# Four copies moved from ScalarE to VectorE, one scaling moved the other way, and a running maximum joined with its new rows, at the end of an attention with soft MoE slots

## The chip, the cores and the metric

The kernel runs on one core of a Trainium2 chip. What counts is the device time of one launch in microseconds. A profiled execution gives, beside its own time, a span: from its first to its last instruction on the core.

## The reference

The inputs are q, k and v of shape (8, 12, 448, 64), a matrix phi of 768 x 32, and the weights w1 (8 experts, 768 x 1024) and w2 (8 experts, 1024 x 768), all float32. What is computed, cut to what matters:

```python
scores = scale * np.matmul(q, k.transpose(0, 1, 3, 2))
m = np.max(scores, axis=-1, keepdims=True)
e = np.exp(scores - m)
attn = e / (np.sum(e, axis=-1, keepdims=True) + np.exp(-m) + 1e-09)
attn_out = np.matmul(attn, v)
x = attn_out.transpose(0, 2, 1, 3).reshape(B * S, H * D)      # 3584 x 768

logits = x @ phi                                              # 3584 x 32
d = np.exp(logits - logits.max(0, keepdims=True))             # over all tokens
d /= d.sum(0, keepdims=True) + 1e-09
slot_input = (d.T @ x).reshape(E, S_per_e, D)                 # 8 experts, 4 slots each
for e in range(E):
    slot_out[e] = np.maximum(slot_input[e] @ w1[e], 0.0) @ w2[e]
c = np.exp(logits - logits.max(1, keepdims=True))             # over the slots
c /= c.sum(1, keepdims=True) + 1e-09
out = c @ slot_out
```

The maximum over all tokens is kept as a running maximum from batch to batch, as in an online softmax.

## The kernel before, in words

The 12 heads of each of the 8 batches are taken two at a time. So there are 48 pairs of heads, numbered 0 to 47, six to a batch (`PB`), three to a group (`NP`). One pair has 448 queries and keys in chunks of 128, 128, 128 and 64; the last half chunks of the two heads share one tile of 128 partitions, one head in each half.

The main loop (L658) runs over the pairs s, with two halves y = 0 and 1. The order of the instructions is written out by hand: each engine does its instructions in the order in which the program issues them. For a pair n:

- `A` and `A1` (L247, L271) compute scores and take their maxima over keys on VectorE (L280, L269), several pairs ahead. `W1`, `W2` and `W3` (L283, L305, L313) negate the maxima of a group on GpSimd (L286), transpose them on TensorE (L309, L310) and copy them to the tile `mT` (L315). `W3` also computes the exponentials of the negated maxima (L318, L321).
- `AB` (L354) computes scores again, transposed: `scores(1)`, `scores(0)` (L366), then `less(1)`, `less(0)` subtract the maxima by a second product with `mT` (L370), and ScalarE takes the exponential (L372). `Bk` (L325) does the same for the half chunk (L344, L347, L350).
- `AV` (L393) multiplies the exponentials with v (L405). Column 64 of every slot of its result is the sum of the exponentials. For pair s, key chunks 0 and 1 are done in its own half y = 1, the rest in the next pair's half y = 0.
- `N1` (L411) copies the result from PSUM to `ubuf` (L417). `N2` (L420) divides: sum and reciprocal on VectorE (L426, L427), then three operations that scale into the tile x: chunks 0 to 2 (L431), the reciprocal spread over two columns of which a mask `halfm` keeps one in each half of the partitions (L435), and the half chunk, with zeros in the other head's columns (L436). From pair 44 on (`on_pool` false) all of it is on VectorE, before that the copy is on ScalarE and the scaling on GpSimd. The last pair is scaled straight from PSUM.
- `PX` (L450) transposes x by four products with the identity (L457) and copies the result to `xT` (L463). In the loop `PX(s - 2)` comes in the half y = 1, after the batch's step of that half. For the last pair it uses two banks and two copies, L460 on ScalarE and L461 on VectorE.

PSUM has three pools: `psA` (three banks: maxima, and the batches' steps), `psB` (four banks, taken in turn by `AB`, `Bk`, `W2`, `PX`), `psV` (one bank, for `AV`).

`P(b)` (L470) is the soft MoE part of batch b, in steps that are put into the dictionary `post` and issued in the halves of later pairs: logits (`l_mm`, L483; copy L496), their maxima over slots (`c_max`, L500), a transposed copy and its maximum over tokens (`l_turn`, L510), `s_max` (a product with the identity spreads the maxima over all partitions, L520; reduction over the four chunks, L521; joined with the old running maximum, L523), `d_sub` (L527), exponentials (L532), the correction of the old sums (`corr`, L537; `fade`, L542), the weighted sums (`s_mm`, L551; `s_add`, L565), and `c_turn` (L556 to L561). For batch 6, the last but one, five steps lie in the second half of pair 43, the two of pair 44 and the two of pair 45.

For the last batch the steps come after the loop: `last[0]` computes logits and transposed logits (`t_mm`, L491) from chunks 0 to 3 of `xT`, `last[1]` from chunk 4, and `last[2]` from chunk 5, after which it does all the rest up to the slots' inputs. In between stand `N1(47)`, `N2(47)`, `PX(46)` and `PX(47)` (L742 to L754). `keep_busy` (L443) issues products whose results are not used.

Then come the experts: `hidden` (L764), `turn`, `slots`, `pick`, and the output's products and scalings (L814 to L879). Weights are loaded by GpSimd's and SyncE's queues during the pairs (`load_half`, `load_first` L131, `load_second` L141), some of them into space that the attention gives free at its end.

Of the kernel before, what the change touches and what calls it, by code (L numbers as in the profile page):

```python
# [8 lines left out]
F32 = mybir.dt.float32  # L9
BF16 = mybir.dt.bfloat16  # L10
AX = mybir.AxisListType
# [20 lines left out]
def kernel(  # L32
# [10 lines left out]
    nc = tc.nc  # L43
# [99 lines left out]
    with ExitStack() as at:  # L143
# [168 lines left out]

        def W3(g):  # L313
            t = psm.tile([128, S], BF16, tag="mT", name="mT")
            nc.scalar.copy(t, st["ps_m"][:, 0:S])  # L315
            mT[g] = t
            e = psm.tile([128, NP, 7], F32, tag="ec", name="ec", bufs=3)
            nc.scalar.activation(e[:, :, 0:6].rearrange("p l (i h) -> p i l h", i=3),  # L318
                                 ngm[g][:, 0:18].rearrange("p (i l h) -> p i l h", i=3, h=2),
                                 AF.Exp, scale=scale)  # L320
            nc.scalar.activation(e[:, :, 6], ngm[g][:, 18:21], AF.Exp, scale=scale)  # L321
            ec[g] = e
# [97 lines left out]
        def N2(n):  # L420
            g, pl = divmod(n, NP)
            b, pb = divmod(n, PB)
            u = us[n]
            eng = nc.gpsimd if on_pool(n) else nc.vector
            rec = psm.tile([128, 7], F32, tag="rec", name="rec", bufs=3)
            nc.vector.scalar_tensor_tensor(rec, u[:, :, D], 1e-9, ec[mg(n)][:, pl, :], op0=ALU.add, op1=ALU.add)  # L426
            nc.vector.reciprocal(rec, rec)  # L427
            x = xb[b % 2]
            c = pb * 128
            rec2 = psm.tile([128, 2], F32, tag="rec2", name="rec2", bufs=3)  # L430
            eng.tensor_mul(  # L431
                x[:, 0:3, c:c + 128].rearrange("p i (h d) -> p i h d", h=2),
                u[:, 0:6, 0:D].rearrange("p (i h) d -> p i h d", h=2),
                rec[:, 0:6].rearrange("p (i h) -> p i h", h=2).unsqueeze(3).to_broadcast([128, 3, 2, D]))
            eng.tensor_scalar(rec2, halfm, rec[:, 6:7], None, op0=ALU.mult)  # L435
            eng.tensor_mul(  # L436
                x[:, 3, c:c + 128].rearrange("p (h d) -> p h d", h=2),
                u[:, 6, 0:D].unsqueeze(1).to_broadcast([128, 2, D]),
                rec2.unsqueeze(2).to_broadcast([128, 2, D]))
# [3 lines left out]
        def keep_busy(n):  # L443

            if "idle" not in st:
                st["idle"] = pb_("ps_idle")
            for _ in range(n):
                nc.tensor.matmul(st["idle"], ident, w_sb["w1", 0][:, 0, 0:512], start=True, stop=True)

        def PX(n):  # L450
            b, pb = divmod(n, PB)
            x, c = xb[b % 2], slice(pb * 128, pb * 128 + 128)
            two = n == NPAIR - 1
            pss = [pb_("ps_x") for _ in range(1 + two)]
            for i in range(4):
                o = (i % 2 if two else i) * 128
                nc.tensor.matmul(pss[i // 2 if two else 0][:, o:o + 128], x[:, i, c], ident if i < 3 else ident2,  # L457
                                 start=True, stop=True)
            if two:
                nc.scalar.copy(xT[:, pb, 0:256], pss[0][:, 0:256])  # L460
                nc.vector.tensor_copy(xT[:, pb, 256:512], pss[1][:, 0:256])  # L461
            else:
                nc.scalar.copy(xT[:, pb, :], pss[0])  # L463

# [3 lines left out]
        def P(b):  # L470
# [7 lines left out]
            def l_mm(js):  # L478
                if js[0] == 0:
                    v["ps_l"] = pa([128, 4, NS], F32, "ps_l")  # L480
                for j in js:
                    for i in range(4):
                        nc.tensor.matmul(v["ps_l"][:, i, :], xT[:, j, i * 128:(i + 1) * 128], phi_sb[:, j, :],  # L483
                                         start=(j == 0 and i == 0), stop=(j == KC - 1), skip_group_check=True)
# [29 lines left out]
            def c_sub():  # L514
                eng.tensor_sub(v["z"][:, 0:4, :], l[:, 0:4, :],
                               v["cm"].unsqueeze(2).to_broadcast([128, 4, NS]))

            def s_max():
                ps = pa([128, 128], F32, "ps_bc")
                nc.tensor.matmul(ps, v["sm"].to_broadcast([128, 128]), ident, start=True, stop=True)  # L520
                nc.vector.reduce_max(new, ps.rearrange("p (i s) -> p s i", i=4), axis=AX.X)  # L521
                if b:
                    nc.vector.tensor_max(new, new, l[:, 4, :])  # L523

            def d_sub():
# [59 lines left out]
            if b < B - 1:  # L585
                steps = [both(lambda: l_mm(range(KC)), l_ev, c_max), both(l_turn, c_sub), both(s_max, d_sub),
                         both(exps, corr), both(s_mm, fade, s_add), c_turn]
                return steps if b < B - 2 else steps[:4] + [both(*steps[4:])]
            return [lambda: (l_mm(range(PB - 2)), t_mm(range(PB - 2))),
                    lambda: (l_mm([PB - 2]), t_mm([PB - 2])),  # L590
                    both(lambda: l_mm([PB - 1]), lambda: t_mm([PB - 1]), l_ev, l_turn, lambda: keep_busy(1), s_max,
                         d_sub, lambda: exps(4, 8), corr, lambda: keep_busy(4), fade, s_last, c_max, c_sub,
                         lambda: exps(0, 4)),
                    c_turn]
# [63 lines left out]
        for s in range(NPAIR):  # L658
            for y in range(2):
                hs = 2 * s + y  # L660
                early = int(hs < 5)
                if early:
                    As(1)
                    Bk(s, 2 * y)
                    As(1)
                    Bk(s, 2 * y + 1)
                    As(1)
                elif s < NPAIR:
                    AB(s, 2 * y)
                    if y:  # L670
                        Bk(s, 3, 1)
                    else:
                        AB(s, 1)
                if hs == 1:
                    W1(1)
                if hs < 5:
                    T(hs + 3)
                if y == 0:
                    if 0 <= s - 1:
                        for i in (2, 3):  # L680
                            AV(s - 1, i, range(3))
                else:
                    if 2 <= s < NPAIR - 6:
                        T(s + 6)
                    g = (s + 1) // 3
                    if (s + 1) % 3 == 0 and g < NG:
                        W2(g + 1)
                        W3(g + 1)
                    if s < NPAIR:
                        for i in (0, 1):  # L690
                            AV(s, i, range(3))
                if 2 * s + y in post:
                    post[2 * s + y]()
                if hs == 2 * (NPAIR - 2) + 1:
                    nc.vector.reduce_max(fold, ident.rearrange("p (i s) -> p s i", i=4), axis=AX.X)
                if y and 0 <= s - 2 < NPAIR - 2 and s - 2 != n6:
                    PX(s - 2)
                if hs == 2 * n6 + 4:
                    PX(n6)
                if y == 0:  # L700
                    if 0 <= s - 1:
                        for i in range(4):
                            AV(s - 1, i, [3])
                        N1(s - 1)
                        if not on_pool(s - 1):
                            N2(s - 1)
                else:
                    if 0 <= s - 1 and on_pool(s - 1):
                        N2(s - 1)
                As(early)  # L710
                if hs == 1:
                    W2(1)
                    W3(1)
                if hs == 4:
                    W1(2)
            g = (s + 10) // 3
            if s == 1 or s % 3 == 2:
                g = 3 if s == 1 else g
                if (s == 1 or g > 3) and g < NG:
                    load(g, "q")  # L720
                    load(g, "k")
            g = (s + 9) // 3
            if s % 3 == 0 and g - 2 < NG:
                V(g - 2)
                if s and g - 1 < NG:
                    load(g - 1, "v")
            if s % 3 == 1:
                if 1 < (s + 2) // 3 < NG:
                    W1((s + 2) // 3 + 1)
                if s == 1:  # L730
                    load(2, "v")
            if s in half_at:
                load_half(half_at[s], 0, w_tile(half_at[s]))
            if s - 2 in half_at:
                load_half(half_at[s - 2], 1)
            if s in narrow_at:
                narrow(narrow_at[s])
            for i, z0, z1 in part_at.get(s, ()):
                load_part(i, z0, z1)
            for i, z0, z1 in col_at.get(s, ()):  # L740
                load_first(i, z0, z1)
# [168 lines left out]
```

## Time and profile before

| | |
|---|---|
| median of 3 runs | 307.56 us (307.03 to 309.63) |
| the profiled execution, its own time | 307.67 us |
| its span | 305.9 us |
| TensorE busy | 274.5 us, 5077 matmuls |
| VectorE busy | 257.0 us, 608 instructions |
| ScalarE busy | 249.7 us, 552 instructions |
| GpSimd busy | 202.8 us, 400 instructions |
| mean granted TensorE clock | 0.963 (1.00 from 230 to 280 us) |

Times in the profile count from the start of the span. Busy time of TensorE is modelled, so that 90% is not its peak. PE is TensorE, DVE VectorE, ACT ScalarE, POOL GpSimd, SP SyncE; PEld is the load of weights into TensorE. A line of the timeline gives start, duration, engine, line of the program, operation, tiles and shapes; in brackets stands how long the engine had been idle before, and what ended it. The duration of an instruction holds a tail in which the next one has already begun, so the distance from start to start is shorter.

### The profile page before, as it was taken

The numbers are of one execution on the slowest core, as the hardware profiler recorded it, in microseconds if no ns is written. First come the engines' busy times: TensorE is split into PE (matmuls) and PEld (weight loads), VectorE is DVE, ScalarE is ACT, GpSimd is POOL, SyncE is SP. The second block draws the span as 40 slices with busy tenths as digits, with TensorE's granted clock in tenths as the row PEclk, the third lists the DMA queues.
The fourth block names the chain that finished last, engine by engine and source line by source line (L and its number), as shares of the span: only waits on it lengthen the run. The fifth ranks groups of instructions, "written<-read, shape, count | busy, mean of one in ns | idle before, by whom it ended". The sixth has DMA issues, their size and how long they took to land.

```text
span 305.9 us, 12225 instructions
## 1 busy us (share of the span) xinstructions
PE 274.5 (90%) x5077; PEld 157.9 (52%) x5078; DVE 257.0 (84%) x608; ACT 249.7 (82%) x552; POOL 202.8 (66%) x400
## 2 busy tenths in 40 slices
PE   7878999999999999999999999999999899994810
PEld 3334565566566656555666556556565555441200
DVE  5989999999999999989999999999999476536930
ACT  2656799999999999989999999999999997335810
POOL 8692788888698869877889697979584862000000
PEclk9999999999999999999999999999999999999555
DMA  6999999999999999998999999999962899927997
GB/s 84 156 149 197 131 207 145 208 182 191 169 192 174 189 181 182 169 204 142 134 170 187 176 189 180 176 189 201 162 90 35 137 135 210 343 106 274 410 441 315
DMA packets 49350, 57.44 MB, mean 188 GB/s; under 512 B 2832, under 2 KB 41488, under 8 KB 48912
## 3 DMA queue, kind: packets, MB, share of 16 engines
q0 software_dynamic: 45536, 42.52, 90.7%
q1 hardware_dynamic: 3760, 14.16, 11.6%
q8 instruction: 39, 0.64, 0.8%
q14 instruction: 15, 0.12, 0.1%
HBM read 88.18 MB, written 14.16 MB: 335 GB/s over the span
## 4 chain that ended last, share of the span: by engine, by line
PE 47%; DVE 27%; POOL 8%; ACT 7%; issue 5%; DMA 2%; DVEq 0%; POOLq 0%
DVE mx L280 14%; PE ps_av L405 11%; PE ps_a L278 6%; PE ps_b L366 5%; PE ps_t L234 4%; PE ps_b L370 4%; PE ps_b L344 3%; DVE mx L269 2%; DMA R<-in_v_dram 2%; DVE W L824 2%; PE ps_x L457 2%; PE ps_so L787 2%; PE ps_h L771 2%; DVE mx L260 2%; DVE R L239 2%
## 5 line engine op out<-in xcount | busy, mean ns | idle before, releaser
L280 DVE TENSOR_REDUCE mx<-ps_a 128x1 f32<-128x448 f32 x252 | 138.9, 614 | 5.4 <-PE ps_a L278 5.1
L372 ACT ACTIVATE R<-ps_b 128x448 bf16<-128x448 f32 x272 | 130.8, 571 | 0.8 <-PE ps_b L370 0.5
L278 PE MATMUL ps_a<-R 64*128 64x448 bf16 x252 | 82.1, 352 | 2.0 <-DVE mx L280 1.8
L366 PE MATMUL ps_b<-R 64*128 64x448 bf16 x272 | 74.2, 353 | 0.9
L370 PE MATMUL ps_b<-mT,sel 64*128 64x448 bf16 x272 | 70.9, 350 | 0.0
L405 PEld LDWEIGHTS <-R 128*128 128x128 bf16 (+1 forms) x1536 | 50.2, 100 | 30.4 <-issue 26.3
L405 PE MATMUL ps_av<-R 128*128 128x65 bf16 (+1 forms) x1536 | 64.5, 196 | 0.0
L431 POOL TENSOR_TENSOR R<-ubuf,rec 128x384 bf16<-128x384 f32 x44 | 36.4, 827 | 35.7 <-DVE rec L427 18.8
L350 ACT ACTIVATE R<-ps_b 128x448 bf16<-128x448 f32 x64 | 35.6, 576 | 3.3 <-PE ps_b L347 3.3
L234 PEld LDWEIGHTS <-R 64*64 64x64 bf16 x1344 | 29.7, 110 | 14.6 <-issue 6.1
L463 ACT CAST R<-ps_x 128x512 bf16<-128x512 f32 x47 | 28.1, 597 | 6.2 <-PE ps_x L457 6.2
L234 PE MATMUL ps_t<-ident,R 64*64 64x64 bf16 x1344 | 31.0, 194 | 1.7 <-DMA R<-in_k_dram 0.4
L269 DVE TENSOR_REDUCE mx<-ps_a 128x1 f32<-128x448 f32 x48 | 29.6, 616 | 0.0
L370 PEld LDWEIGHTS <-sel 64*128 64x128 bf16 x272 | 21.5, 94 | 14.6 <-issue 5.0
L278 PEld LDWEIGHTS <-R 64*128 64x128 bf16 x252 | 23.6, 94 | 10.0
L417 ACT COPY ubuf<-ps_av 128x455 f32<-128x455 f32 x44 | 25.2, 573 | 3.0 <-PE ps_av L405 2.8
L237 ACT COPY R<-ps_t 128x896 bf16<-128x896 bf16 x20 | 18.4, 922 | 9.0 <-PE ps_t L234 8.7
L260 DVE TENSOR_REDUCE mx<-ps_a 128x1 f32<-128x448 f32 x36 | 20.5, 618 | 3.6 <-PE ps_a L256 3.4
L344 PE MATMUL ps_b<-R 64*64 64x448 bf16 (+1 forms) x112 | 21.6, 371 | 0.0
L347 PE MATMUL ps_b<-mT,sel 64*64 64x448 bf16 (+1 forms) x112 | 20.4, 349 | 0.1
L436 POOL TENSOR_TENSOR R<-ubuf,rec 128x128 bf16<-128x128 f32 x44 | 17.6, 400 | 3.7
L366 PEld LDWEIGHTS <-R 64*128 64x128 bf16 x272 | 17.3, 94 | 4.7 <-issue 0.2
(136 smaller groups left out, 456.1 us busy)
## 6 DMA issues: line engine op xcount, KB each, us to landing
W<-in_moe_w_dram POOLq DMA_DIRECT2D x22, 768.0 KB, 9.6
R<-in_v_dram POOLq DMA_DIRECT2D x32, 192.0 KB, 5.2
out_dram<-W SPq DMA_DIRECT2D x2, 2688.0 KB, 10.3
R<-in_q_dram POOLq DMA_DIRECT2D x15, 336.0 KB, 7.2
R<-in_k_dram POOLq DMA_DIRECT2D x15, 336.0 KB, 8.1
wd<-in_moe_w_dram POOLq DMA_DIRECT2D x8, 384.0 KB, 10.2
R<-wd SPq DMA_DIRECT2D x8, 384.0 KB, 8.4
R<-in_moe_w_dram POOLq DMA_DIRECT2D x2, 768.0 KB, 9.2
```

The source lines that it names most:

```text
L234: nc.tensor.transpose(ps[r, a, c:c + 64], src[r, pl, tok * D:(tok + 1) * D], ident[r, r])
L269: nc.vector.reduce_max(mx[g][:, c:c + 1], ps[:, 0:S], axis=AX.X)
L278: nc.tensor.matmul(ps[:, 0:S], t[r, 0, i * 128:(i + 1) * 128], t[r, 1, :], start=True, stop=True)
L280: nc.vector.reduce_max(mx[g][:, c:c + 1], ps[:, 0:S], axis=AX.X)
L344: nc.tensor.matmul(outs[hl], t[rs[hl], 1, cols], t[rs[hl], 0, :], start=True, stop=False)
L350: nc.scalar.activation(e, p[:, 0:S], AF.Exp, scale=scale)
L366: nc.tensor.matmul(ps[hl][:, 0:S], t[rs[hl], 1, cols], t[rs[hl], 0, :], start=True, stop=False)
L370: nc.tensor.matmul(ps[hl][:, 0:S], sel[rs[hl], h:h + 1].to_broadcast([64, 128]), mT[mg(n)][rs[hl], :], start=False, stop=True)
L372: nc.scalar.activation(e[:, hl, :], ps[hl][:, 0:S], AF.Exp, scale=scale)
L405: nc.tensor.matmul(o, eT[n, i, hl][:, qc], vp[g % 2][:, 2 * pl + hl, i, 0:W65], start=(i == 0 and u == 0 and hl == 0), stop=(i == 3), skip ...
L431: eng.tensor_mul(x[:, 0:3, c:c + 128].rearrange("p i (h d) -> p i h d", h=2), u[:, 0:6, 0:D].rearrange("p (i h) d -> p i h d", h=2), rec[: ...
L463: nc.scalar.copy(xT[:, pb, :], pss[0])
```

## The change

1. `W3` of the last group (pairs 45 to 47) copies the transposed maxima (128x448) on VectorE instead of ScalarE.
2. `PX` of pairs 42, 43 and 44 copies its result (128x512) on VectorE instead of ScalarE.
3. In `N2` of the last pair, the masked reciprocal and the masked scaling of the half chunk on VectorE are replaced by two scalings of 64 partitions x 64 columns on ScalarE, each into its own head's columns. The other head's columns are set to zero beforehand by two memsets on GpSimd, issued at pair 45.
4. For the last batch, a new step `old_max`, issued in `last[0]`, copies the running maximum to bf16 on VectorE and brings it by a product with the identity into 32 columns beside those that the spread maxima will take. `s_max` then reduces over five rows instead of four, and the operation that joined the old maximum (L523) is gone in the last batch.
5. In `last[2]`, the transposed logits of chunk 5 are computed before the logits instead of after them.

```diff
         def W3(g):
             t = psm.tile([128, S], BF16, tag="mT", name="mT")
-            nc.scalar.copy(t, st["ps_m"][:, 0:S])
+            (nc.vector.tensor_copy if g == NG else nc.scalar.copy)(t, st["ps_m"][:, 0:S])
...
+            if n == NPAIR - 1:
+                for hl in range(2):
+                    r = slice(64 - 64 * hl, 128 - 64 * hl)
+                    nc.scalar.mul(x[r, 3, c + 64 * hl:c + 64 * hl + 64], u[r, 6, 0:D], rec[r, 6:7])
+                return
             eng.tensor_scalar(rec2, halfm, rec[:, 6:7], None, op0=ALU.mult)
...
             else:
-                nc.scalar.copy(xT[:, pb, :], pss[0])
+                (nc.vector.tensor_copy if NPAIR - 6 <= n < NPAIR - 3 else nc.scalar.copy)(xT[:, pb, :], pss[0])
...
+            def old_max():
+                t = psm.tile([128, NS], BF16, name="omax", bufs=1)
+                nc.vector.tensor_copy(t, l[:, 4, :])
+                v["ps_bc"] = pa([128, 5 * NS], F32, "ps_bc")
+                nc.tensor.matmul(v["ps_bc"][:, 128:5 * NS], ident, t, start=True, stop=True)
+
             def s_max():
-                ps = pa([128, 128], F32, "ps_bc")
-                nc.tensor.matmul(ps, v["sm"].to_broadcast([128, 128]), ident, start=True, stop=True)
-                nc.vector.reduce_max(new, ps.rearrange("p (i s) -> p s i", i=4), axis=AX.X)
-                if b:
+                n = 5 if "ps_bc" in v else 4
+                ps = v["ps_bc"] if "ps_bc" in v else pa([128, 128], F32, "ps_bc")
+                nc.tensor.matmul(ps[:, 0:128], v["sm"].to_broadcast([128, 128]), ident, start=True, stop=True)
+                nc.vector.reduce_max(new, ps.rearrange("p (i s) -> p s i", i=n), axis=AX.X)
+                if b and n == 4:
                     nc.vector.tensor_max(new, new, l[:, 4, :])
...
-            return [lambda: (l_mm(range(PB - 2)), t_mm(range(PB - 2))),
+            return [lambda: (l_mm(range(PB - 2)), t_mm(range(PB - 2)), old_max()),
                     lambda: (l_mm([PB - 2]), t_mm([PB - 2])),
-                    both(lambda: l_mm([PB - 1]), lambda: t_mm([PB - 1]), l_ev, l_turn, lambda: keep_busy(1), s_max,
+                    both(lambda: t_mm([PB - 1]), lambda: l_mm([PB - 1]), l_ev, l_turn, lambda: keep_busy(1), s_max,
...
+                if hs == 2 * (NPAIR - 3):
+                    c = 128 * (PB - 1)
+                    for hl in range(2):
+                        nc.gpsimd.memset(xb[(B - 1) % 2][64 * hl:64 * hl + 64, 3, c + 64 * hl:c + 64 * hl + 64], 0.0)
```

## The prediction, on record before the result

> **What bounds the kernel now.** I read the page first, then the timeline of the span between 232 and 272 us, where all of the change lies, then the chain of waits over the same stretch, then the groups kept apart by shape, for prices. The profiled execution took 307.67 us (span 305.9); the median of the three runs is 307.56, so a sum against the one is 0.1 high against the other.
>
> ```profile
> span 305.9 us, 12225 instructions
> PE 274.5 (90%) x5077; PEld 157.9 (52%) x5078; DVE 257.0 (84%) x608; ACT 249.7 (82%) x552; POOL 202.8 (66%) x400
> ```
>
> These shares say little about the last four pairs, where VectorE has no more maxima to take (its tenths fall from 9 to between 3 and 7). There ScalarE works almost without a pause:
>
> ```profile
> 249.45 2.96 ACT L372 ACTIVATE R<-ps_b 128x448 bf16<-128x448 f32 x6
> 252.30 0.55 ACT L350 ACTIVATE R<-ps_b 128x448 bf16<-128x448 f32 x1
> 252.73 0.60 ACT L463 CAST R<-ps_x 128x512 bf16<-128x512 f32 x1
> 253.19 3.00 ACT L372 ACTIVATE R<-ps_b 128x448 bf16<-128x448 f32 x6
> ```
>
> From 249.45 to 253.19 one pair costs 3.74 us on ScalarE: seven exponentials and the copy at L463, which takes a place of 0.46 us. The reader should see that L463 is no mere burden of ScalarE. The chain of waits goes through it into TensorE:
>
> ```profile
> 252.85 0.49 ACT R L463
> 253.38 0.35 PE ps_b L366
> 253.92 0.72 PE ps_av L405 x20
> ```
>
> Banks of psB are handed out in turn, four of them. After PX(s-2) has taken one, the next pair's AB(s+1,0) takes two and AB(s+1,1) two more, and the last of these, scores(0), gets the bank that PX's copy has to empty. The trace shows that at each pair: copies end at 245.21, 249.56 and 253.33, and the second score product of the next AB starts at 245.25, 249.61 and 253.38. So **the moment at which the PX copy ends releases TensorE**, which then does the subtractions (L370), the 20 products of AV (L405), and so releases N1 on VectorE. The change moves this copy to another queue; what stands in that queue ahead of it decides.
>
> ```profile
> 244.39 0.29 DVE L521 TENSOR_REDUCE lb<-ps_bc 128x32 f32<-128x128 f32 x1 [2.30 <-PE ps_bc L520]
> 245.19 0.16 DVE L426 SCALAR_TENSOR_TENSOR rec<-ubuf,ec 128x7 f32<-128x7 f32 x1
> 250.10 0.18 DVE L561 RECIPROCAL crec<-crec 128x4 f32<-128x4 f32 x1
> 250.97 0.63 DVE L417 COPY ubuf<-ps_av 128x455 f32<-128x455 f32 x1 [0.69 <-PE ps_av L405]
> 253.02 0.36 DVE L695 TENSOR_REDUCE ubuf<-ident 128x32 f32<-128x128 bf16 x1
> ```
>
> In program order the copy of PX(42) comes after L527 and before L426, that of PX(43) after L561 (the end of the seventh batch's steps), that of PX(44) after L695. VectorE is gapless from L417 at 246.62 to 250.28 and from 250.97 to 253.38, so these are the ends of full queues.
>
> **Prices.** VectorE's copies from PSUM with a cast:
>
> ```profile
> L791 DVE CAST W<-ps_so 128x384 bf16<-128x384 f32 x2 | 1.1, 558 | 1.8 <-PE ps_so L787 1.8
> L461 DVE CAST R<-ps_x 128x256 bf16<-128x256 f32 x1 | 0.4, 425 | 0.3 <-PE ps_x L457 0.3
> ```
>
> That is 1.04 ns a column, so 0.69 for 512 columns (0.60 on ScalarE) and 0.625 for 448 (0.53 at L315).
>
> **Pair 44.** ScalarE loses L315 (0.43 to the next start) and a L463. On VectorE the copy of the maxima's rows starts when L310 has ended, 243.97, and ends at 244.60; L521 starts at 244.63 to 244.68 instead of 244.39. L521, L523 and L527 take the 0.80 us they took, so the PX(42) copy runs from 245.45 to 246.14, where ScalarE had it done at 245.21: **+0.93**. The first exponential of pair 45 gains nothing: L370 needs mT, 0.10 later than now. L426 and L427 of N2(43) move behind the copy, and POOL's L431 with them, from 245.74 to 246.7. POOL was idle for 0.88 us after N2(43), before its weight loads at 248.20, and in this gap the two new memsets go (0.21 for 128x128 at L757, so at most 0.45 the two). The four loads then leave up to 1 us later; they land in 9 to 10 us, and are read after 271. Nothing for the sum; without the 10 us of cover it would be 1. No other transfer is moved past: SP's eight loads from 255.90 go out when the last products have read their space, and shift with them.
>
> **Pair 45.** TensorE is 0.93 late, so AV(44) and N1(44) are. From there VectorE's ops run back to back through L561, so the copy of PX(43) starts at 250.26 + 0.93 and ends 0.69 later, 251.88; ScalarE had it at 249.56 (2.32 late). This pair alone adds 0.70 + 0.69 = **+1.39**. The copy waits behind twelve VectorE instructions that start only after AV(44) has ended; scores(0) of AB(46,1) waits for the copy, behind it in TensorE's queue the 20 products of AV(45), and for these N1(45).
>
> **Pair 46.** N1(45), N2(45) and the fold at L695 all follow at the same distance, and the copy of PX(44) can start when L695 ends, at 253.35 + 2.32, and ends 0.69 later; ScalarE's ended at 253.33, before L695 did. **+0.71**, together **+3.03**.
>
> The relief of ScalarE, four places of 0.43 to 0.47, 1.85 us, is spent waiting: with scores(0) of AB(47,1) at 256.4, its exponentials start 2.7 late, and the next, for AB(47,2), again when TensorE's L370 has ended (255.11 now, 258.15 then). L350 of the last pair moves from 256.08 to 259.1, and with it N2(47). Bounds of this term: below, if the three copies took no time (three times 0.69 and the 0.24 of mT come off), +0.7; above, if the copies cost 0.90 each, as ScalarE's L822 does for 768 columns, and mT as much more, +3.9. I take 3.03, because the two rows it is drawn from are of the same engine, memory and type.
>
> **The end of the attention.** Times here are those of the trace before, the shift left out.
>
> ```profile
> 257.62 0.59 ACT L463 CAST R<-ps_x 128x512 bf16<-128x512 f32 x1 [0.52 <-PE ps_x L457]
> 260.00 0.29 DVE L510 TENSOR_REDUCE sm<-ps_lT 128x1 bf16<-128x128 f32 x1 [0.49 <-PE ps_lT L491]
> 260.62 0.29 DVE L521 TENSOR_REDUCE lb<-ps_bc 128x32 f32<-128x128 f32 x1 [0.32 <-PE ps_bc L520]
> 260.94 0.19 DVE L523 TENSOR_TENSOR lb<-lb,lb 128x32 f32<-128x32 f32 x1
> 261.24 0.33 DVE L527 TENSOR_TENSOR z<-lb,lb 128x160 f32<-128x160 f32 x1
> ```
>
> The last pair's half chunk leaves VectorE (L435 and L436, 0.22 and 0.29) and becomes two 64x64 scalings on ScalarE, ahead of the copy of PX(46) in ScalarE's order. They wait for the reciprocal, which ends at 257.70, while that copy starts at 257.62 now. ScalarE's small instructions follow each other by 0.10 to 0.22 (L321 to L463, L532 to L537), and a scale that is read from a tile adds 0.1 (L822 0.585, L791 0.479, both 384 columns). I take 0.22 each (0.10 to 0.33): the copy starts at 258.18, **+0.56** (0.3 to 0.8). The Trainium skill (ScalarE: Activation LUTs, What ACT_TABLE_LOAD costs) gives 186 ns plus 0.833 ns a column, 93 ns more for a pointer operand and 93 ns of overlap; the pair of rows agrees with the pointer's price, and the copy would by it start at 258.22. Behind it wait the products of chunk 4 (258.26 now), then PX(47). The removed L436 ended at 258.75, before PX(47) will now need it: it gives nothing back.
>
> With the transposed products of chunk 5 first, L510 no longer waits for four products of L483 (259.38 to 259.71), but two of its own then wait for VectorE's half of the copy: **-0.25** (0 to -0.33). Old and new maxima in one reduction: L521 to L527 takes 0.62, and becomes 0.35, for 32 columns more: **-0.27**. Its copy and its product lie between L431 and chunk 4, and TensorE waits there for PX(46) anyway; uncovered they would cost 0.2. Sum of the end: **+0.04** (-0.4 to +0.5).
>
> In all 307.67 + 3.03 + 0.04 = 310.74, and 0.1 less against the median: I say **310.7 us**.
>
> **Rivals.** 1. *ScalarE's relief decides, faster.* Should VectorE have each copy done no later than ScalarE had, pairs 45 to 47 run at ScalarE's pace, 3.28 instead of 3.74, and the four places of 1.85 us come off: 305.8. It decides from the point where the copy ends before scores(0) is due. For it: VectorE is idle for 1.03, 0.69 and 1.30 us in these pairs. Against: these gaps lie before N1, not where the copy stands in the order. 0.12.
>
> 2. *Only part of the delay arrives.* If the first 0.93 is absorbed, as TensorE and ScalarE both waited some 0.3 us around 248.9, and half of the next: 309.1. Against: no gap of VectorE lies between 246.62 and 250.28. 0.12.
>
> 3. *TensorE's clock falls.* The granted clock is 1.00 up to 280 us and 0.85 from 280 to 285, where TensorE is busy for 2.43 of 5 us. With waits of up to 1.8 us it would be busy some 60% in the late pairs. At half speed for 5 us, 3 us of products take 3 more, of which I let two thirds through: 312.7. Against: from 275 to 280 it was busy 2.99 of 5 at 1.00. The Trainium skill (TensorE: Matmul & The Clock Gate, Part 1: The HAM clock gate) has the clock fall after an idle window of about 3.4 us; by that it stays up here, and the trace agrees with it as far as 280. 0.06.
>
> **How the numbers follow.** The forecast has 0.70, with its own range 309.7 to 311.6. Between 306.4 and 312.4 lie the forecast, rival 2, and what of the others comes near: 8 in 10. One per cent, about what a measurement of this kernel can tell from no change, is 3.1 us, and the forecast lies on it: of its 0.70 I put 0.42 above 310.64, since each stage has a new wait between engines, and 0.28 below. Slower by over 1%: 0.42 + 0.06 = 0.48. Faster by over 1% needs 304.5, which even rival 1 misses by 1.3: 0.03. Within 1%: 0.49.
>
> **What would show it.** Right: in the chain of waits the new 512-column copies on VectorE, 0.65 to 0.72 each, each followed at once by the second L366 of an AB; ScalarE with gaps of 0.5 to 2 us before exponentials of pairs 45 to 47; the last L350 near 259.1; no maximum of its own (L523) in the last batch and L521 to L527 at 0.35. Wrong: ScalarE without gaps from 245 to 256, or the last exponential before 256.1; then rival 1 holds. A granted clock under 1.00 before 270 would mean rival 3.

## The result, and the profile after

The changed kernel is slower: the ratio of its times to those of the kernel before is 1.0107 (95% interval 1.0073 to 1.0142). The medians are 312.14 us against 309.86, nine runs each; their quotient alone is 1.0074, at the lower end of the interval. The forecast of 310.7 against 307.56 is a ratio of 1.0102. So the size of the loss is near the forecast, but by luck: it is made from two sums, and by the profiles below the one for the pairs is 1.52 us too high and the one for the end 0.85 too low. In microseconds, 312.14 lies above the range of 309.7 to 311.6; the kernel before, too, measured 2.30 more here than the 307.56 from which that range was worked out.

The profiled execution after took 312.83 us, its span is 311.1. The span is 5.2 us longer, but not all of that is the change. The token maximum of pair 44 (L510, after: L515) is the last landmark ahead of the first changed instruction; in the fence it stands first before, then after.

```profile
241.47 0.29 DVE L510 TENSOR_REDUCE sm<-ps_lT 128x1 bf16<-128x128 f32 x1 [0.58 <-PE ps_lT L508]
244.23 0.29 DVE L515 TENSOR_REDUCE sm<-ps_lT 128x1 bf16<-128x128 f32 x1 [0.58 <-PE ps_lT L513]
```

So 2.76 us lie in unchanged code. Of these, 1.85 are there already at the first copy of N1 (at 25.0 before); TensorE's granted clock was 0.50 from 17.25 to 24.08 in the profile after, and 1.00 there in the one of before. The other kernels below have the landmark anywhere from 241.96 to 244.58. From here on every reading is therefore a stretch between two landmarks of the same trace:

| stretch, us | before | after |
|---|---|---|
| pairs: token maximum of pair 44 to the last pair's sum from PSUM | 15.83 | 17.34 |
| end 1: that sum to the last batch's token maximum | 2.70 | 3.79 |
| end 2: that maximum to the first sum of the slots' inputs | 2.56 | 2.36 |
| the experts, to the second cast of the slots' outputs on VectorE | 14.97 | 14.97 |
| the output, to the end of the span | 28.37 | 28.41 |
| all | 64.43 | 66.87 |

The change costs 1.51 us in the pairs and 0.89 in the two stretches of the end. The 2.44 us in all are 0.8% of the time, within the interval.

The next fence is VectorE's timeline after. Its columns are start, duration, engine and line, operation, and in brackets the idle time before. It answers to the VectorE lines shown of before.

```profile
246.72 0.62 DVE L315 CAST mT<-ps_m 128x448 bf16<-128x448 f32 x1 [1.88 <-PE ps_m L310]
247.26 0.28 DVE L533 TENSOR_REDUCE lb<-ps_bc 128x32 f32<-128x128 f32 x1
...
248.04 0.68 DVE L468 CAST R<-ps_x 128x512 bf16<-128x512 f32 x1
...
253.57 0.66 DVE L468 CAST R<-ps_x 128x512 bf16<-128x512 f32 x1
...
256.92 0.68 DVE L468 CAST R<-ps_x 128x512 bf16<-128x512 f32 x1
```

The copies of PX (L468) stand where the prediction put them, at the end of a full queue: VectorE is not idle before any of them. They and the copy of the maxima's rows (L315) take what it said, 0.66 to 0.68 and 0.62. The copies of PX end at 248.72, 254.23 and 257.60. Now TensorE, whose second score product (L366) of an AB block was to wait for them:

```profile
248.43 0.35 PE L366 MATMUL ps_b<-R 64*128 64x448 bf16 x1 [0.44 <-ACT R L372]
...
253.23 0.35 PE L366 MATMUL ps_b<-R 64*128 64x448 bf16 x1 [0.44 <-ACT R L372]
...
257.65 0.35 PE L366 MATMUL ps_b<-R 64*128 64x448 bf16 x1 [0.78 <-DVE R L468]
```

Only the third waits for its copy. The first two start before the copy has ended and are released by an exponential. In the program as built, the banks of psB came strictly in turn before, through all 423 allocations. After, they do so except at these two places: there scores(0) is given the bank of the same pair's first score block, and the bank of the copied ps_x goes to the next block.

Now the end of the attention. Of before, the last pair's sum and the products of chunk 4:

```profile
257.30 0.17 DVE L426 SCALAR_TENSOR_TENSOR rec<-ps_av,ec 128x7 f32<-128x7 f32 x1 [0.49 <-PE ps_av L405]
...
258.26 0.27 PE L483 MATMUL ps_l<-phi_sb,R 128*128 128x32 bf16 x4
```

And the end after, over all engines:

```profile
261.57 0.17 DVE L426 SCALAR_TENSOR_TENSOR rec<-ps_av,ec 128x7 f32<-128x7 f32 x1 [0.49 <-PE ps_av L405]
261.77 0.20 DVE L427 RECIPROCAL rec<-rec 128x7 f32<-128x7 f32 x1
262.00 0.56 DVE L431 TENSOR_TENSOR R<-ps_av,rec 128x384 bf16<-128x384 f32 x1
...
262.66 0.63 ACT L438 ACTIVATE R<-ps_av,rec 64x64 bf16<-64x64 f32 x2 [1.28 <-DVE omax L525]
...
263.19 0.56 ACT L468 CAST R<-ps_x 128x512 bf16<-128x512 f32 x1
263.81 0.27 PE L488 MATMUL ps_l<-phi_sb,R 128*128 128x32 bf16 x4 [0.93 <-ACT R L468]
...
265.98 0.32 DVE L533 TENSOR_REDUCE lb<-ps_bc 128x32 f32<-128x160 f32 x1 [0.32 <-PE ps_bc L532]
266.40 0.33 DVE L539 TENSOR_TENSOR z<-lb,lb 128x160 f32<-128x160 f32 x1
```

The two scalings (L438) do not start when the reciprocal is done (261.97) but 0.69 later, when VectorE's L431 has ended (262.56). The line names L525 as the releaser; in the program as built, the first scaling waits for the semaphore count that L431 raises, one below that of L525. Scalings and L431 read the same bank, ps_av; that this is why they are kept apart was not varied in a run. From the start of the first scaling to the start of the copy of PX(46) it is 0.53 us. The products of chunk 4 (L488) follow the last pair's sum by 2.24 us (261.57 to 263.81); before it was 0.96 (257.30 to 258.26).

### The profile page after: what moved, and what is told of

Read it like the earlier page. It is cut to its first block, busy times and chain, and to the rows that moved or that the text cites. A ratio compares the mean times of both kernels' runs of the same rounds, so it can differ in the third digit from the quotient of the medians.

```text
span 311.1 us, 12232 instructions
## 1 busy us (share of the span) xinstructions
PE 277.1 (89%) x5078; PEld 158.9 (51%) x5079; DVE 258.9 (83%) x610; ACT 249.1 (80%) x550; POOL 202.3 (65%) x402
## 4 chain that ended last, share of the span: by engine, by line
PE 49%; DVE 27%; ACT 7%; POOL 5%; issue 4%; DMA 3%; DVEq 0%; POOLq 0%
DVE mx L280 14%; PE ps_av L405 11%; PE ps_a L278 6%; PE ps_b L366 5%; PE ps_t L234 5%; PE ps_b L370 4%; DMA R<-in_k_dram 3%; PE ps_b L344 3%; DVE mx L269 2%; PE ps_o L832 2%; DVE mx L260 2%; PE ps_so L803 2%; PE ps_h L787 2%; PE ps_x L462 2%; DVE R L239 2%
## 5 line engine op out<-in xcount | busy, mean ns | idle before, releaser
L366 PE MATMUL ps_b<-R 64*128 64x448 bf16 x272 | 74.3, 353 | 2.4 <-ACT R L372 0.9
L431 POOL TENSOR_TENSOR R<-ubuf,rec 128x384 bf16<-128x384 f32 x44 | 36.3, 825 | 40.1 <-DVE rec L427 23.5
L468 ACT CAST R<-ps_x 128x512 bf16<-128x512 f32 x44 | 26.3, 598 | 6.2 <-PE ps_x L462 6.2
L344 PE MATMUL ps_b<-R 64*64 64x448 bf16 (+1 forms) x112 | 22.7, 383 | 0.0
L347 PE MATMUL ps_b<-mT,sel 64*64 64x448 bf16 (+1 forms) x112 | 21.4, 360 | 0.0
L366 PEld LDWEIGHTS <-R 64*128 64x128 bf16 x272 | 17.4, 94 | 4.7 <-issue 0.2
```

The source lines that it names most:

```text
L344: nc.tensor.matmul(outs[hl], t[rs[hl], 1, cols], t[rs[hl], 0, :], start=True, stop=False)
L366: nc.tensor.matmul(ps[hl][:, 0:S], t[rs[hl], 1, cols], t[rs[hl], 0, :], start=True, stop=False)
L431: eng.tensor_mul(x[:, 0:3, c:c + 128].rearrange("p i (h d) -> p i h d", h=2), u[:, 0:6, 0:D].rearrange("p (i h) d -> p i h d", h=2), rec[: ...
```

## The experiments

Stretches are those of the table above. Line numbers in a trace are those of its own kernel.

**The copies of PX back on ScalarE**, all else as changed.

```diff
-                (nc.vector.tensor_copy if NPAIR - 6 <= n < NPAIR - 3 else nc.scalar.copy)(xT[:, pb, :], pss[0])
+                nc.scalar.copy(xT[:, pb, :], pss[0])
```

> The changed kernel with the three copies of PX(42) to PX(44) back on ScalarE; the rest of the change stays. The measure is the stretch from the start of the token maximum of pair 44 (241.47 in the profile before, 244.23 after) to the end of the span: 64.4 us before, 66.9 after. Theory A (read from the two traces): the copies on VectorE cost 1.4 of the 2.4 us, the scalings on ScalarE 0.9 net of what the joined maximum and the order give back. It expects 65.4 here, and the whole time 0.3 to 0.6% above before. Theory B (the prediction): all of the loss comes with the copies on VectorE, the end is even: 64.5 to 64.6, within 0.1% of before. Theory C: the copy of the maxima's rows on VectorE alone makes the pairs late: 66.5, 0.9% above.

Measured: pairs 15.83, exactly as before; end 1 3.79 and end 2 2.36, as after; all 65.34. The ratio is 1.0039 (0.9997 to 1.0081). Theory A holds. The copies of PX cost the whole 1.51 of the pairs, and the copy of the maxima's rows, which is still on VectorE here, costs nothing by itself: theory C falls, and theory B with it.

**The half chunk scaled by VectorE again**, all else as changed (the block with `nc.scalar.mul` and the two memsets are taken out).

> The changed kernel with the last half chunk scaled by VectorE again (and no memsets); the rest stays. Theory A: the 1.28 us that the products of chunk 4 are late at the end come off, of which up to 0.2 stays because TensorE then waits for the copied old maximum: stretch 65.6 to 65.8, 0.4 to 0.5% above before. Theory B (the end is even): 66.9, 1.0% above before.

Measured: pairs 17.36, end 1 3.15, end 2 2.36, all 66.22; ratio 1.0085 (1.0048 to 1.0123). Only 0.64 comes off, against the 1.07 to 1.27 of theory A and the nothing of theory B: something else in end 1 is now in the way.

**Joined maximum and order alone**, on the kernel before.

> Before with two parts of the change alone: the old maximum joined in the reduction, and the transposed logits of chunk 5 first. Theory A: 0.20 from the removed maximum and 0.19 from the order, as the trace after shows them: stretch 64.0, ratio 0.9987. The prediction's own sizes (0.27 and 0.25, with up to 0.2 lost where TensorE waits for the copied maximum) give 63.9 to 64.1. A rival: TensorE waits for the copied maximum and for the bank it takes, and nothing is gained: 64.4.

Measured: pairs 15.83, end 1 3.21, end 2 2.78, all 65.18, ratio 1.0037 (0.9999 to 1.0074). It misses all that was expected: the two parts that were to gain lose 0.5 in end 1. The lines of VectorE and TensorE say why:

```profile
259.42 0.17 DVE L520 CAST omax<-lb 128x32 bf16<-128x32 f32 x1
259.64 0.18 PE L522 MATMUL ps_bc<-omax,ident 128*128 128x32 bf16 x1 [0.58 <-DVE omax L520]
```

The copy of the old maximum stands behind all of N2(47) in VectorE's order. Its product stands ahead of the products of chunk 4 and of PX(47) in TensorE's, so both wait for a value that has been ready since pair 44. The kernel with the scaling back on VectorE has the same wait, and that is what was in its way. In the changed kernel TensorE is held by PX(46) anyway, and the wait is hidden. End 2 is longer here for another reason; in the fence are the stretches of 2 us in which it lies (busy time of the engines PE, PEld, DVE, ACT and POOL, then the granted clock, DMA share and GB/s):

```profile
260.00:262.00 2.00, 1.63 (x18) 1.04 (x16) 0.72 (x2) 0.64 (x2) 0.00 (x0) 0.72 1.17 312
262.00:264.00 2.00, 1.80 (x21) 0.97 (x21) 1.04 (x3) 0.43 (x2) 0.00 (x0) 0.50 1.12 315
```

TensorE's granted clock fell to half in this execution, from 260.88 on, which it did not at this place in the profiles of before and after. It is also the likely reason why end 1 is 0.06 longer here than with the scaling back on VectorE (3.21 against 3.15).

**The banks in turn.** The changed kernel with four tags of one bank each, so that the turn is fixed.

```diff
-        pb_ = lambda nm: psB.tile([128, 512], F32, tag="b", name=nm)
+        bank = [0]
+
+        def b_tag():
+            bank[0] += 1
+            return f"b{(bank[0] - 1) % 4}"
+
+        pb_ = lambda nm: psB.tile([128, 512], F32, tag=b_tag(), name=nm)
```

> The changed kernel with the four banks of psB named one by one and taken strictly in turn. In the profile before they came in turn everywhere; after, the second score product of AB(45,1) and of AB(46,1) waits for an exponential of the same pair instead of for the copy of PX. Theory A: this other order of banks is what halved the loss that the prediction gave to the pairs (3.0 forecast, 1.5 seen). In turn, scores(0) waits for the copies again and the pairs lose 3.0: stretch 68.3 to 68.5, 1.5% above before. Rival: the order of banks makes no difference, since VectorE's queue sets the pace either way: 66.9, 1.1%.

Measured: pairs 18.56, which is 2.73 over before; ratio 1.0136 (1.0083 to 1.0189). The second score products now wait as the prediction had it:

```profile
247.27 0.35 PE L372 MATMUL ps_b<-R 64*128 64x448 bf16 x1 [0.78 <-DVE R L474]
...
252.93 0.35 PE L372 MATMUL ps_b<-R 64*128 64x448 bf16 x1 [1.31 <-DVE R L474]
...
257.35 0.35 PE L372 MATMUL ps_b<-R 64*128 64x448 bf16 x1 [0.78 <-DVE R L474]
```

All three are released by the copy on VectorE. So the order of the banks is what took 1.2 us (18.56 to 17.34) off the loss. All in all 68.80 against the 68.3 to 68.5 expected; the clock fell in this profile too, to 0.50 from 266 to 268, and end 2 and the experts are 0.26 and 0.46 longer than after. Without these 0.72 it would be 68.08, just under what was expected.

**The scaling on ScalarE alone**, on the kernel before.

> Before with one part of the change alone: the last half chunk scaled by ScalarE, with the memsets. Measure: the stretch from the start of the last pair's sum (reading PSUM, 257.30 in the profile before) to the start of the last batch's token maximum: 2.70 before, 3.79 after. Theory A: ScalarE's two scalings wait for the end of VectorE's three-chunk scaling (L431), which reads the same bank of PSUM, and stand ahead of the copy of PX(46): 3.98, that is 1.28 more than before, ratio 1.004. Rival D: they wait for the copy of the old maximum, as the list of waits after has it; without that copy they start when the reciprocal is done, 0.6 to 0.7 earlier: 3.3. Theory B (the prediction): 0.56 more, 3.26.

Measured: ratio 1.0051 (1.0020 to 1.0082). End 1 is 4.32, but in this profile the clock falls at 262.73, so only what lies before that is read:

```profile
261.50 0.63 ACT L438 ACTIVATE R<-ps_av,rec 64x64 bf16<-64x64 f32 x2 [1.28 <-DVE R L431]
...
262.65 0.28 PE L488 MATMUL ps_l<-phi_sb,R 128*128 128x32 bf16 x4 [1.23 <-ACT R L468]
```

The last pair's sum starts at 260.41, so the scalings start 1.09 and the products of chunk 4 2.24 behind it, both to the hundredth as after. Here is no copied old maximum, and L431 is named as releaser: rival D falls. The 1.28 of theory A is measured; the prediction's 0.56 is not.

**The scalings behind the copy of PX(46).** The same part alone, but `PX(n - 1)` is issued between the rest of N2(47) and the two scalings.

> The same part alone, but with the two scalings issued behind the copy of PX(46) in ScalarE's order. Theory A (place in ScalarE's queue is what costs): 2.65 to 2.80, as before. Rival: the scalings as such are late, wherever they stand, since VectorE's L436 ended earlier than two of them can: 3.0 or more.

```profile
258.73 0.59 ACT L469 CAST R<-ps_x 128x512 bf16<-128x512 f32 x1 [0.52 <-PE ps_x L463]
...
259.44 0.63 ACT L439 ACTIVATE R<-ps_av,rec 64x64 bf16<-64x64 f32 x2
...
259.74 0.69 PE L463 MATMUL ps_x<-ident,R 128*128 128x128 bf16 x4
```

Measured in one execution: end 1 2.98, just under the rival's bound and 0.28 over before. The place in the queue was most of the price, 1.00 of 1.28. The rest stays: the last product of PX(47) (at 260.21) is released by the second scaling, which ends 1.66 behind the last pair's sum, where L436 ended 1.45 behind it.

**The copies left out.**

The diff is cut to the copies; the tags of one bank each are those of the kernel with the banks in turn.

```diff
-                nc.scalar.copy(xT[:, pb, :], pss[0])
+                if not NPAIR - 6 <= n < NPAIR - 3:
+                    nc.scalar.copy(xT[:, pb, :], pss[0])
```

> Before without the copies of PX(42) to PX(44) (the last batch's logits then use stale rows for three of six column chunks), with psB's banks strictly in turn, as they were. It gives the most that taking these copies from ScalarE could bring. Measure: from the start of the token maximum of pair 44 to the start of the last pair's sum, 15.83 before. Theory E: each copy lies in the time in which TensorE computes the next pair's first scores, which the exponential behind it waits for anyway: 15.4 to 15.8. Rival 1 of the prediction (ScalarE's relief counts in full): 14.4.

Measured in one execution: pairs 14.81, 1.02 less than before. Neither theory E (at most 0.4) nor the rival (1.4) is right. ScalarE's exponentials of pairs 45, 46 and 47:

```profile
247.31 1.85 ACT L378 ACTIVATE R<-ps_b 128x448 bf16<-128x448 f32 x4 [0.38 <-PE ps_b L376]
...
251.34 2.73 ACT L378 ACTIVATE R<-ps_b 128x448 bf16<-128x448 f32 x6 [0.46 <-PE ps_b L376]
...
254.62 2.77 ACT L378 ACTIVATE R<-ps_b 128x448 bf16<-128x448 f32 x6
```

Measured from the token maximum of pair 44, they start 3.62, 7.65 and 10.93 us in; before it was 3.63, 7.98 and 11.72. Without its copy, pair 45 gains nothing: ScalarE waits 0.38 for TensorE's L376, which is the subtraction. Pair 46 gains 0.33, and a wait of 0.46 is left in place of a copy of 0.48. Only pair 47 gains a whole place.

**The joined maximum without the late wait**: before, with the order of the last logits and the joined maximum, but the copy issued at pair 46 and the product at pair 47.

> Before with the joined maximum and the order of the last transposed logits, but the copy of the old maximum issued at pair 46 and its product at pair 47, where nothing waits for them. Theory A: the gain of 0.19 by the order and 0.19 by the maximum is kept and the 0.65 that TensorE waited for the late copy goes: 2.51 from the last pair's sum to the last token maximum (2.70 before, 3.21 with the late copy), then 2.36 to the first sum of the slots' inputs (2.56 before) where the granted clock stays at 1.00; the whole 0.4 less, ratio 0.9988. Rival: the gain is lost again behind it, and the time is as before: ratio 1.000.

Measured: pairs 15.83, end 1 2.53, end 2 2.36, all 64.05, each within 0.02 of theory A. So the order gives 0.17 and the joined maximum 0.20, as after, where the reduction and L539 start 0.42 apart (265.98 to 266.40) instead of 0.62. The ratio, 1.0006 (0.9978 to 1.0033), cannot tell 0.38 us from nothing, nor from the rival; the stretches can.

**One copy on VectorE, in a better place**, on top of the version before this one.

The diff is cut: the tags of one bank each are left out, and so are the parts of the version before.

```diff
-                nc.scalar.copy(xT[:, pb, :], pss[0])
+                (nc.vector.tensor_copy if n == NPAIR - 4 else nc.scalar.copy)(xT[:, pb, :], pss[0])
...
                     AB(s, 2 * y)
+                    if hs == 2 * (NPAIR - 2) + 1:
+                        PX(s - 2)
+                        N2(s - 1)
...
-                if y and 0 <= s - 2 < NPAIR - 2 and s - 2 != n6:
+                if y and 0 <= s - 2 < NPAIR - 2 and s - 2 != n6 and s != NPAIR - 2:
                     PX(s - 2)
...
-                        if not on_pool(s - 1):
+                        if not on_pool(s - 1) and s != NPAIR - 2:
                             N2(s - 1)
```

> The version early_max (joined maximum, its copy early, order of the last logits), with one of the three copies on VectorE, that of PX(44), in a better place: its products right behind the first score block of pair 46, its copy ahead of N2(45) in VectorE's order instead of behind it and the fold; psB's banks strictly in turn. Measure: from the start of the token maximum of pair 44 to the start of the last pair's sum, 15.83 before, 14.81 with all three copies left out. Theory E (a copy taken from ScalarE brings what TensorE does not hold up anyway, if it ends before the bank is needed): the copy ends near 252.7 on the clock of the profile before, where ScalarE's ended at 253.33; the first exponential of pair 47 then waits for L370 at 253.01 instead of 253.19 for ScalarE: 15.65, and the whole 0.5 to 0.6 under before, ratio 0.998. Rival (VectorE's queue is too full for any of these copies; N2(45) or N1(46) is late): 16.0 or more.

```profile
253.34 0.69 DVE L469 CAST R<-ps_x 128x512 bf16<-128x512 f32 x1
...
254.59 0.35 PE L372 MATMUL ps_b<-R 64*128 64x448 bf16 x2
...
254.79 2.73 ACT L378 ACTIVATE R<-ps_b 128x448 bf16<-128x448 f32 x6 [0.31 <-PE ps_b L376]
```

Measured: pairs 15.50, all 63.68, which is 0.75 under before; ratio 0.9948 (0.9922 to 0.9975), faster than both kernels. The 0.75 us are 0.24% of the time; the interval lies just beyond that, and what the runs gain beyond the stretches is not explained here. The copy ends at 254.03 and the second score product that needs the bank starts at 254.59 without a wait. Theory E's sign holds, its size (15.65) was 0.15 short, and its path is only a part of it. The first exponential of pair 47 starts 11.67 behind the landmark, 0.05 earlier than before and not the 0.18 forecast: in place of the copy stands a wait of 0.31 for TensorE. The larger part comes from TensorE, which is no longer held by the copy: from the first of the pair's six exponentials to the start of the one of the half chunk (257.34) it is 2.55 us, where before it was 2.89 (253.19 to 256.08). So a copy on VectorE that cost time at the end of the queue can gain time further ahead in it. The products of PX(44) were moved forward as well, and no run has ScalarE's copy in this place, so what the engine gave and what the place gave are not separated.

## Why the prediction was right or wrong

**What bounds the pairs: right.** ScalarE works almost without gaps before, and the end of the PX copy releases TensorE. With the banks in turn the chain of waits is the one that was written down, link by link.

**The pairs, 3.03: wrong by half, 1.51.** The step that failed is "Banks of psB are handed out in turn, four of them". That was read from the profile before and taken over to the changed kernel; there the turn is broken at two of the three places, just where the copy went to VectorE. With the turn held the arithmetic was near. N1 of pairs 44, 45 and 46, counted from the landmark, is late by 0.78, 2.09 and 2.73 us, where the sum had 0.93, 2.32 and 3.03; after, it is late by 0.42, 0.86 and 1.51. So after, the first 0.86 come from two waits for an exponential and only the last 0.65 from waiting for a copy on VectorE. In the sum itself the first term was the one over-sized most, 0.78 for 0.93: the copy of the maxima's rows holds VectorE for 0.54 from start to start (246.72 to 247.26 after), where the sum took its whole duration.

**ScalarE's relief, "spent waiting": right in sign.** Nothing of it is seen after, where the first exponentials of pairs 45 and 46 wait 0.82 and 0.95 for TensorE. But its worth was put at 1.85 with the four places counted in full. The three copies, 1.42 by that count, are worth 1.02 when they are left out altogether, and that holds what TensorE gains by no longer waiting for them. The rest lies in the time in which TensorE's subtraction is awaited in any case.

**The end, +0.04: wrong, 0.89.** Three terms were mis-sized. The scalings were given 0.56 and cost 1.28: the step that failed is "they wait for the reciprocal". They wait for L431, 0.69 behind the reciprocal, and from the first scaling to the copy it is 0.53, not 0.44. The order of the logits was given 0.25 and gives 0.17, the joined maximum 0.27 and gives 0.20. The old maximum's wait, costed at 0.2 without its cover, costs 0.62 without it, the difference between end 1 of the kernel with the scaling on VectorE (3.15) and of the one with the early copy (2.53).

**The rule on ScalarE's instructions.** By the figures of the Trainium skill (ScalarE: Activation LUTs, What ACT_TABLE_LOAD costs) the distance from one 64-column scaling with a pointer operand to the next is, as an estimate, 0.24 us, which makes 0.48 for the two. Measured are 0.32 from the first to the second and 0.21 from there to the copy, 0.53 in all, nearer to it than the 0.44 of the sum. That section says nothing on the wait, which cost more than the instructions.

**The rivals.** Rival 2, a part of the delay, has the right size for the pairs, for a reason it did not name. Rival 1, a relief of 1.85, did not happen and could not have in full: all three copies left out give 1.02, and one in a better place on VectorE 0.33. Rival 3, the clock, did not happen in the profile after (1.00 up to 285 us), but did in three of the experiments, behind the pairs, not within them.

**The chances.** The forecast lay on the bound of one per cent and the chances were split accordingly, 0.49 for within and 0.48 for slower; the interval leaves no doubt that it is slower, while its size remains about one per cent.

## What to carry to other kernels

A copy out of a rotating buffer is part of the chain of whoever needs the buffer next, so before moving it to a less busy engine, look at what stands ahead of it in that engine's order, not at the engine's share. When an edit changes which engine frees a buffer, read again from the changed program which buffer the next user gets: the turn seen before need not survive. A small instruction put ahead of a copy on the critical chain is priced by what it waits for, and two engines that read one PSUM bank may be made to wait for each other, as the scalings waited for L431 here (0.69 us).

## What the runs showed of the hardware that was not expected

TensorE's granted clock fell to 0.50 behind the pairs in three profiles: for 3.41 us from 260.88 in the kernel with the joined maximum and the order alone, for 3.41 from 265.53 with the banks in turn, and for 6.83 from 262.73 with the scaling alone. In the clock records of all eleven traces, every stretch of one clock except the last of a trace is a multiple of 3.41 us. TensorE had not been idle for long: in the 3.41 us ahead of each fall it was busy for 2.49, 2.02 and 2.18, with longest waits of 0.58, 0.93 and 1.23. After, with 2.21 of 3.41 busy from 263.01 on and a longest wait of 0.93, the clock stayed at 1.00. So neither the busy time, as the profile models it, nor the longest wait tells a fall from none. The rule of the Trainium skill that was cited in rival 3 (TensorE: Matmul & The Clock Gate, Part 1: The HAM clock gate), an idle window of about 3.4 us, has the length of these steps, but does not cover the falls as it was used, as a bound on single waits. What decides was not settled here. Where a fall came, end 2 and the experts together were longer by 0.42, 0.72 and 1.03 us than in the profile of after (the first two) or of before (the third).
